# Left operands of the last three FFN2 blocks moved to the first weights' buffers, with order lists made anew

## The chip, the cores and the metric

The kernel runs on one core of one Trainium2 chip. The metric is the device time of one execution in microseconds (us), taken as the median over several runs. A profile of one execution comes with it. Engines are named as in the profile: PE (TensorE matmuls) and PEld (its weight loads), DVE (VectorE), ACT (ScalarE), POOL (GpSimd) and SP (the queue that issues nearly all DMAs).

## The reference

One transformer block with modulation: S = 2048 tokens, D = 512, attention with 32 heads in four segments, then a feed-forward part with F = 1792. Only the second part matters here:

```python
def _B_ref(x, w1, b1, w2, b2):
    h = jnp.einsum("bsd,df->bsf", x, w1) + b1
    r = jnp.where(h > 0, h, 0)
    h = r * r
    return jnp.einsum("bsf,fd->bsd", h, w2) + b2
...
h = _layernorm(x, axis=-1) * (1 + cb) + sb
x = x + gb * _B_ref(h, B_w1, B_b1, B_w2, B_b2)
```

## The kernel before

The tokens are worked through in four stages of 512 (s = 0 to 3). Attention comes first; the feed-forward part fills the second half of the run, and the attention of late stages is mixed into its start.

**Precision.** Each fp32 operand of a product is split into a rounded part and a remainder, and a product is three matmuls (high by high, high by low, low by high). "Splitting" is a cast on ACT and a subtraction on DVE.

**FFN1** (`ffn1(s, p)`, p = 0 to 6) makes 256 hidden columns for 512 tokens with a Strassen-like scheme: seven products m1 to m7 instead of eight. A product is six matmuls of 128x256 (`bh` in the profile, line 1652). DVE adds the products up (lines 1664 and 1668), ACT or DVE applies the squared ReLU (lines 1682, 1685, 1686). The result is X(s, p, i), where i = 0, 1 is the half of the tokens.

**FFN2** (`ffn2(s, i, p)`) multiplies X(s, p, i) by 256 rows of the second weights and sums over the seven blocks p in four PSUM banks, one for each *group* of products: g0 = products 1 and 6, g1 = 7 and 5, g2 = 3 and 4 (six matmuls each), g3 = product 2 (three matmuls). That is 21 matmuls for a block (`bm`, line 1737). Each block needs a left operand first:

- four sums s1 to s4 of 128x128 on POOL (line 1714);
- `hr`, the cast of three pieces (128x384) on ACT (line 1721), and `lr`, its remainder on DVE (line 1722);
- `hs`, the cast of the four sums (128x512) on ACT (line 1724), and `ls`, its remainder on DVE (line 1725).

All four splits write one buffer of the pool `ao`. It has two buffers, and one comes free when all four groups of its block are done. After the last block ten additions on DVE (lines 1769, 1771, 1773; `acc` in the code) add the four banks to two 128x512 tiles `ya` and `yb`, which hold the residual; POOL has added the bias to these (line 1752). Then they go out by DMA (line 1788). In the very last half (s = 3, i = 1) `ya` goes out in two pieces.

Which group an addition needs: a1 and a6 need g0; a7 and a5 need g1; a3 and a4 need g2; a2 needs g3. `yb` gets a1, a6, a7, a5, a4; `ya` gets a1, a6, a5, a3, a2.

**First weights.** `fetch_w1` loads w1 for FFN1 into a pool `w1` of three buffers (two inside the tile ST, one called w1c), in two pieces h = 0, 1 for each block.

**Order.** The order of the work on each engine is written out as lists of node numbers (`ORDER`); a planner (`Plan.run`) follows the list of each engine strictly and hands out buffers of the pools on the way. An engine waits at the head of its list, even when a later entry could run.

Of the kernel before, what the change touches and what calls it, by code (L numbers as in the profile page):

```python
# [17 lines left out]
P = 128  # L18
# [50 lines left out]
1113 1450-1451 1203 1211 1117-1119 1121 1362 1453 1128 1199 1454 1214 1136 1455 1124 1217 1131 1456 1359 1317 1365  # L69
# [6 lines left out]
1701 1609 1830 1704 1793 1610 1708 2051 1711 2052 1799 1716 2053 1688 2054 1806 1612 1820 1720 1833 1721-1722 1814  # L76
# [5 lines left out]
2462 2267 2463 2009 2464 2246 2243 2465 2013-2014 2249 2159 2015 2166 2162 2017 2169 1968 2178 2276 2174 2252 2599  # L82
# [15 lines left out]
3464-3465 3519 3516 3479-3481 3518 3517 3483 3482 3531 3529 3484 3528 3530 3543 3542 3751 3541 3540 3553 3750 3555  # L98
3554 3552 3749 3752 3567 3755 3565 3564 3754 3566 3576 3578 3769 3753 3577 3770 3579 3775 3771 3773 3772 3605-3607
3774 3604 3619 3616-3618 3790 3628 3631 3629 3789 3630 3791 3641 3794 3793 3642 3640 3795 3792 3643 3809 3655  # L100
3652-3654 3811 3810 3664 4099 3812 3667 4094 3676 3813-3814 3665 3677 4084 3666 3815 4089 3679 3678 3827-3831 3833
3832 3892 3890 3848 3847 3904 3845 3889 3846 3891 3901 3850-3851 3863 3866 3864-3865 3902-3903 3849 3916 3913 3867
3915 3868 3928 3914 3926-3927 3869 4134 3925 4137 4136 4135 3938 4138 3940 3937 3939 4154-4155 4157 4140 4139 4156
3950 3952 3949 3961 3951 4158 3964 4159 3962-3963 4160 4174 4176 3991 3989 3992 4177 4175 4179 3990 4003 4178 4001
4194 4004 4002 4014 4180 4016 4015 4013 4195-4196 4025 4027-4028 4197 4026 4037 4039 4212 4040 4038 4199-4200 4050
4198 4049 4052 4061 4213 4215 4214 4064 4051 4062 4216-4218 4230 4063 4232 4231 4276 4275 4235 4274 4286 4236 4277
4233 4289 4287-4288 4248 4300 4298 4301 4299 4249-4250 4253 4313 4254 4310 4325 4312 4311 4323 4322 4324 4234 4336
4334 4346 4337 4349 4335 4347-4348 4251-4252 4376 4374-4375 4377 4386 4389 4388 4387 4400 4399 4401 4398 4413 4410
4412 4411 4422 4425 4423-4424 4435-4437 4434 4446-4447 4449 4448
# [25 lines left out]
2111-2112 497 1881 1973 1976 1975 1979-1980 1972 2337 1982-1983 1987-1988 240 2133 2132 2342 2261 2260 2348 499 2344  # L135
# [23 lines left out]
700 702 471 470 609 483 608 462 461 467-468 602-603 402-403 597 599-600 855 605 861 639 606 491 629 618 630 1423-1424  # L159
# [34 lines left out]
4203 4046 4048 4058 4207 4204-4205 4060 4208 4206 4070 4220 4069 4072 4071 4211 4271 4273 4221 4225 4073-4074 4222
4226 4283 4075-4076 4078 4229 4223 4077 4285 4238-4239 4243-4244 4247 4224 4297 4295 4309 4241 4307 4319 4256-4257
4321 4261-4262 4265 4240 4331 4333 4343 4345 4242 4354 4356 4355 4357 4371 4373 4360-4361 4363 4358-4359 4383 4362
4385 4258-4260 4395 4397 4407 4409 4419 4421 4431 4433 4443 4445 4455 4454 4457 4460-4461 4463 4456 4458-4459 4462
# [14 lines left out]
2750 2413 2767 2510 2421 2420 2425 2746 2471 2443 2436 2444 2448 2748 2784-2786 2537 2794 2545 2544 2560 2549 2797  # L212
# [1623 lines left out]
```

## Time and profile before

| what | value |
|---|---|
| runs | 741.7, 743.84, 744.1 us, median 743.84 us |
| the profiled execution | 743.41 us, of it span 741.6 us |
| PE busy | 725.6 us (98% of the span) |
| DVE, POOL, ACT busy | 623.1, 493.3, 485.2 us |
| DMA | 151.82 MB, mean 205 GB/s |
| granted TensorE clock | 0.999 |

The span is what the trace covers; the profiled execution's own time is 1.8 us longer. "Busy" counts the time in which an engine had an instruction under way. A line of a timeline gives the start, the length, the engine, the line of the kernel, what is written and read, how many instructions were merged, and in square brackets how long the engine sat idle before and what ended that. The brackets stand only where the wait was worth showing.

### The profile page before, as it was taken

Reading aid. Unit: us, or ns where it says so; the run is one execution under the profiler, and the core shown is the slowest. Engines: PE = TensorE matmul, PEld = TensorE weight load, DVE = VectorE, ACT = ScalarE, POOL = GpSimd, SP = SyncE. Lnnn points to the kernel's source line nnn. Section 1 sums busy time; section 2 is a strip of 40 time slices with the busy share of each in tenths; the row PEclk is TensorE's granted clock in tenths of the full one; section 3 lists DMA queues with packets and bytes.
Section 4 is the critical chain, followed back from the end, with each engine's and each line's share of the span. In section 5 each row is a group of like instructions: output and inputs, shape, how many; then the busy total and the mean of one; then the engine's idle time right before and its main releaser. Section 6 shows DMA issues by size and latency. Waiting matters only on the chain.

```text
span 741.6 us, 20354 instructions
## 1 busy us (share of the span) xinstructions
PE 725.6 (98%) x7405; PEld 615.6 (83%) x7405; DVE 623.1 (84%) x1674; ACT 485.2 (65%) x1070; POOL 493.3 (67%) x675
## 2 busy tenths in 40 slices
PE   8999999999999999999999999999999999999996
PEld 7795777767877677775777789999999999999996
DVE  5588889898899889889998779998798877877885
ACT  3769987998879987788779654674326333643342
POOL 6767846898768787355887564766565825575672
PEclk9999999999999999999999999999999999999999
DMA  9878865437544463448673689899877667677620
GB/s 310 263 196 263 249 184 132 136 103 224 160 128 118 103 173 101 129 118 255 216 243 109 204 293 344 277 318 315 296 247 239 217 230 256 253 246 233 208 72 29
DMA packets 84606, 151.82 MB, mean 205 GB/s; under 512 B 10134, under 2 KB 32666, under 8 KB 84508
## 3 DMA queue, kind: packets, MB, share of 16 engines
q1 hardware_dynamic: 84356, 150.40, 65.0%
q8 instruction: 59, 0.97, 0.5%
q14 instruction: 39, 0.32, 0.1%
q10 hardware_dynamic: 152, 0.13, 0.1%
HBM read 94.14 MB, written 29.36 MB: 167 GB/s over the span
## 4 chain that ended last, share of the span: by engine, by line
PE 85%; DVE 5%; DMA 3%; ACT 3%; issue 1%; POOL 1%; SPq 1%; DVEq 0%; ACTq 0%; POOLq 0%
PE bm L1737 18%; PE bh L1652 18%; PE bqk L868 11%; PE bpv L1204 8%; PE ba L976 6%; PE bpb L1145 6%; PE bv L938 5%; PE bwop L1355 2%; PE bwarm L570 2%; DVE ba L981 1%; DMA ST<-w1d 1%; PE bmr L1069 1%; PE blnq L644 1%; PE blnq L653 1%; DMA ST<-sg 1%
## 5 line engine op out<-in xcount | busy, mean ns | idle before, releaser
L981 DVE CUSTOM_DVE_ANT_0 ba<-ba,msk 128x384 f32<-128x384 f32 (+2 forms) x384 | 192.9, 530 | 26.2 <-PE ba L976 16.5
L1162 ACT ACTIVATE pt<-bpb 128x512 f32<-128x512 f32 x320 | 174.7, 624 | 12.6 <-PE bpb L1145 9.7
L1149 POOL TENSOR_SCALAR_AFFINE_SELECT pt<-pt 128x512 f32<-128x512 f32 x128 | 80.6, 647 | 60.4 <-ACT pt L1162 47.1
L868 PE MATMUL bqk<-HT,WQK 64*128 64x512 f32 x720 | 106.6, 397 | 0.3 <-ACT HT L844 0.3
L1737 PE MATMUL bm<-w,ST 128*128 128x256 f32 x660 | 93.9, 283 | 0.5 <-DVE ST L1725 0.5
L1737 PEld LDWEIGHTS bm<-w,ST 128*128 128x128 f32 x660 | 85.2, 191 | 0.9 <-DVE ST L1725 0.9
L1652 PE MATMUL bh<-ST 128*128 128x256 f32 x594 | 83.4, 283 | 0.4 <-DVE ST L1446 0.4
L1204 PE MATMUL bpv<-pt,VT 128*32 128x512 f32 (+3 forms) x1024 | 82.1, 438 | 0.8 <-POOL pt L1149 0.4
L1145 PE MATMUL bpb<-ST 64*128 64x256 f32 (+2 forms) x512 | 81.5, 347 | 0.7 <-DMA ST<-mt 0.6
L868 PEld LDWEIGHTS bqk<-HT,WQK 64*128 64x128 f32 x720 | 73.4, 185 | 8.6 <-ACT HT L844 0.8
L976 PE MATMUL ba<-ST 63*128 63x256 f32 (+2 forms) x512 | 77.3, 341 | 0.9 <-DMA ST<-sg 0.6
L1652 PEld LDWEIGHTS bh<-ST 128*128 128x128 f32 x594 | 76.4, 190 | 1.3 <-DVE ST L1446 0.6
L976 PEld LDWEIGHTS ba<-ST 63*128 63x128 f32 x512 | 52.5, 185 | 20.6 <-issue 4.6
L1145 PEld LDWEIGHTS bpb<-ST 64*128 64x128 f32 x512 | 53.6, 185 | 16.5 <-issue 3.9
L1204 PEld LDWEIGHTS bpv<-pt,VT 128*32 128x32 f32 x1024 | 27.2, 109 | 33.6 <-issue 22.1
L938 PE MATMUL bv<-WVO,HT 64*128 64x512 f32 x384 | 54.6, 396 | 0.0
L981 DVE DVE_READ_ACCUMULATOR2_ANT mx<- 128x1 f32 x384 | 54.0, 141 | 0.0
L779 POOL TENSOR_TENSOR X1L<-X1L 128x512 fp32r<-128x512 f32 (+1 forms) x28 | 32.2, 1150 | 14.3 <-ACT X1L L778 12.7
L938 PEld LDWEIGHTS bv<-WVO,HT 64*128 64x128 f32 x384 | 38.6, 186 | 3.4
L1009 ACT COPY ac<-ba 128x512 f32<-128x512 f32 x64 | 35.8, 600 | 6.0 <-PE ba L976 5.4
L1020 DVE TENSOR_REDUCE mx<-ac 128x4 f32<-128x1024 f32 x32 | 38.9, 1214 | 0.1
L1652 PE MATMUL bh<-H2o,ST 128*128 128x256 f32 x252 | 35.7, 281 | 1.4 <-DMA ST<-w1d 1.0
(298 smaller groups left out, 1719.5 us busy)
## 6 DMA issues: line engine op xcount, KB each, us to landing
ST<-sg SPq DMA_DIRECT2D x192, 128.0 KB
ST<-w1d SPq DMA_DIRECT2D x21, 1024.0 KB
ST<-w1d SPq DMA_DIRECT2D x19, 768.0 KB
w1d<-X1L SPq DMA_DIRECT2D x21, 512.0 KB
w1c<-w1d SPq DMA_DIRECT2D x7, 1024.0 KB
w1c<-w1d SPq DMA_DIRECT2D x9, 768.0 KB
xt<-in_A_x SPq DMA_DIRECT2D x16, 256.0 KB
wm<-in_w_mod SPq DMA_DIRECT2D x16, 256.0 KB
```

The source lines that it names most:

```text
L868: nc.tensor.matmul(bank(banks[w]), W3(w, k, x, cols.start, cols.stop)[r], HT[r, y, k], start=first and i == 0, stop=last and i == 2)
L938: nc.tensor.matmul(bank(banks[t]), HT[r, x, k, (t2 + t) * P:(t2 + t + 1) * P], WVO[r, k, y], start=first and i == 0, stop=last and i == 2)
L976: nc.tensor.matmul(dst[:, c0:c0 + n], ST[b:b + 63, 0, sl, qt * P:(qt + 1) * P], ST[b:b + 63, 1, sl, :n], start=True, stop=True)
L981: nc.vector.tensor_tensor_reduce(i, i, msk[:, 512 - n:], scale=1.0, scalar=-3e38, op0=ALU.add, op1=ALU.max, accum_out=o)
L1009: cp = [act(512, lambda j=j: nc.scalar.copy(buf("ac", ac)[:, j], bank(keys[j])), pr[0] + 0.01 + 0.001 * j, after=[first], put=[keys[j]]) f ...
L1020: reds.append(op("DVE", 1.13, lambda: nc.vector.tensor_reduce(buf("mx", mx).rearrange("p (a t) -> p a t", t=4)[:, :, 1], acv(), axis=AX.X, ...
L1145: nc.tensor.matmul(dst, ST[b:b + 64, 1, sl, kb * P:(kb + 1) * P], ST[b:b + 64, 0, sl, q0:512], start=True, stop=True)
L1149: nc.gpsimd.affine_select(out=ap, in_=ap, pattern=[[0, ap.shape[1]], [1, P]], compare_op=ALU.is_ge, fill=0.0, base=0, channel_multiplier=-1)
L1162: ns = [op("ACT", 0.49, lambda j=j: nc.scalar.activation(buf("PPP"[n], pt)[:, i + j], bank(keys[j]), AF.Exp, scale=0.25), pr[slot] + 0.01 ...
L1204: nc.tensor.matmul(bank(o)[32 * hq:32 * hq + 32, q0:q0 + src.shape[1]], v[:, a:a + 32], src, start=start, stop=stop, tile_position=(0, 32 ...
L1652: nc.tensor.matmul(pb(i), A[:, x, kk], B[:, y, kk], start=kk == j == 0, stop=kk == 1 and j == 2)
L1737: nc.tensor.matmul(q if wide else q[:, c * HALF:(c + 1) * HALF], TL[ao][a >= 3][:, x, a_ * P:(a_ + 1) * P], LT["w2z"][:, b:15:14 - b] if w ...
```

## The change

1. In the last half (s = 3, i = 1) blocks 4, 5 and 6 write their left operand into a buffer of the pool `w1` instead of `ao`. The same four splits write it, in the same sizes, and the matmuls read it there.
2. `ORDER` is made anew. The lists agree up to small swaps until the end of stage 1 of FFN1; from there they differ on every engine. At the end PE no longer finishes block after block: it does g3 of blocks 2 to 6 last.

No instruction that computes, and no DMA, is added or removed. All lines below the lists move by one up and, from `ffn2` on, by five down (1737 becomes 1742, for example).

```diff
@@ ffn2 @@
-        ao, sk = ("ao", s, i, p), ("S", s, i, p)
+        late = s == NS - 1 and i == 1 and p >= NP - 3
+        ao, sk = ("w1" if late else "ao", s, i, p), ("S", s, i, p)
+
+        def A_(k, x):
+            if late:
+                return FF_w1(ao).rearrange("p h a k n -> p h (a k n)")[:, x, (0, 3 * P)[k]:(3 * P, 7 * P)[k]]
+            return ao_tile(ao)[k][:, x]
...
-        hr = act(384, lambda: nc.scalar.copy(ao_tile(ao)[0][:, 0], X(0, 3)), us(t0 - 5), sbuf=True, after=ready, get=[("ao", ao)])
+        hr = act(384, lambda: nc.scalar.copy(A_(0, 0), X(0, 3)), us(t0 - 5), sbuf=True, after=ready, get=[(ao[0], ao)])
...
@@ ORDER, the end of PE's list @@
-4412 4411 4422 4425 4423-4424 4435-4437 4434 4446-4447 4449 4448
+4412 4410 4422 4411 4424 4434 4436 4423 4446 4435 4447-4448 4401 4413 4425 4437 4449
```

**PE, the end of the program.** The matmuls of the last half, three for a product. The weights' name tells the block: w_7999 is block 2, w_8000 block 3, w_8001 block 4, WVO block 5, w_8795 block 6. Before:

```order
L1737 MATMUL bm<-w_8001,ao 128x256 x3
L1737 MATMUL bm<-w_8001,ST 128x256 x3
L1737 MATMUL bm<-w_8001,ao 128x256 x3
L1737 MATMUL bm<-w_8001,ST 128x256 x9
L1737 MATMUL bm<-w_8001,ao 128x256 x3
L1737 MATMUL bm<-WVO,ST 128x256 x21
L1737 MATMUL bm<-w_8795,ao 128x256 x3
L1737 MATMUL bm<-w_8795,ST 128x256 x9
L1737 MATMUL bm<-w_8795,ao 128x256 x3
L1737 MATMUL bm<-w_8795,ST 128x256 x3
L1737 MATMUL bm<-w_8795,ao 128x256 x3
```

After:

```order
L1742 MATMUL bm<-WVO,w1c 128x256 x12
L1742 MATMUL bm<-w_8001,ST 128x256 x6
L1742 MATMUL bm<-w_8795,ST 128x256 x6
L1742 MATMUL bm<-WVO,w1c 128x256 x6
L1742 MATMUL bm<-w_8795,ST 128x256 x12
L1742 MATMUL bm<-w_7999,ST 128x256 x3
L1742 MATMUL bm<-w_8000,ao 128x256 x3
L1742 MATMUL bm<-w_8001,ST 128x256 x3
L1742 MATMUL bm<-WVO,w1c 128x256 x3
L1742 MATMUL bm<-w_8795,ST 128x256 x3
```

Before, all of block 6 stood at the end, so every bank got its last matmul within the last 21. Now g0 of block 6 has 33 matmuls behind it, g1 21 and g2 15, and the last 15 are g3 of five blocks.

**DVE, the end of the program.** The last remainders of left operands and the ten additions. In the names X1L and Tx_8006 before are `ya` and `yb`; Tx_8009 and Tx_8008 are `ya` and `yb` after. Before:

```order
L1722 TENSOR_TENSOR ST<-T_6303,ST 128x384
L1725 TENSOR_TENSOR ST<-Tx_8009,ST 128x512
L1722 TENSOR_TENSOR ao<-T_6303,ao 128x384
L1725 TENSOR_TENSOR ST<-X1L,ST 128x512
L1769 TENSOR_TENSOR X1L<-bm,X1L 128x512
L1769 TENSOR_TENSOR Tx_8006<-bm,Tx_8006 128x512
L1773 TENSOR_TENSOR X1L<-bm,X1L 128x256 x4
L1769 TENSOR_TENSOR Tx_8006<-bm,Tx_8006 128x512 x2
L1773 TENSOR_TENSOR Tx_8006<-bm,Tx_8006 128x256
L1771 TENSOR_TENSOR Tx_8006<-Tx_8006,bm 128x256
```

After:

```order
L1727 TENSOR_TENSOR w1c<-X1L,w1c 128x384
L1730 TENSOR_TENSOR ST<-T_6295,ST 128x512
L1774 TENSOR_TENSOR Tx_8009<-bm,Tx_8009 128x512
L1778 TENSOR_TENSOR Tx_8009<-bm,Tx_8009 128x256
L1774 TENSOR_TENSOR Tx_8008<-bm,Tx_8008 128x512
L1778 TENSOR_TENSOR Tx_8009<-bm,Tx_8009 128x256
L1774 TENSOR_TENSOR Tx_8008<-bm,Tx_8008 128x512
L1778 TENSOR_TENSOR Tx_8009<-bm,Tx_8009 128x256
L1774 TENSOR_TENSOR Tx_8008<-bm,Tx_8008 128x512
L1778 TENSOR_TENSOR Tx_8008<-bm,Tx_8008 128x256
L1776 TENSOR_TENSOR Tx_8008<-Tx_8008,bm 128x256
L1778 TENSOR_TENSOR Tx_8009<-bm,Tx_8009 128x256
```

The ten additions are the same; they now stand as a1 ya, a6 ya, a1 yb, a5 ya, a6 yb, a3 ya, a7 yb, a5 yb, a4 yb, a2 ya, so `yb` is ready before `ya`, and the last output is the 128x256 half of `ya` instead of the whole `yb`. Both lists have all left operands ahead of the additions.

**POOL, the end of the program.** The sums for left operands (128x128) and the bias additions of the last half (128x512). Before:

```order
L1752 TENSOR_TENSOR Tx_8006<-Tx_8006,WVO 128x512
L1714 TENSOR_TENSOR Tx_8009<-T_6303 128x128
L1714 TENSOR_TENSOR Tx_8008<-X1L,Tx_8008 128x128
L1714 TENSOR_TENSOR Tx_8009<-Tx_8009,T_6303 128x128
L1752 TENSOR_TENSOR X1L<-X1L,WVO 128x512
L1714 TENSOR_TENSOR X1L<-T_6303 128x128
```

After:

```order
L1719 TENSOR_TENSOR Tx_8007<-X1L,Tx_8007 128x128
L1719 TENSOR_TENSOR Tx_8007<-X1L 128x128
L1719 TENSOR_TENSOR T_6295<-T_6295 128x128 x4
L1757 TENSOR_TENSOR Tx_8009<-Tx_8009,WVO 128x512
L1757 TENSOR_TENSOR Tx_8008<-Tx_8008,WVO 128x512
```

The two bias additions stood between the sums of blocks 3, 5 and 6; now they are the last two entries.

More of the change, by code (lines that the diff above doesn't have):

```diff
@@ L102 @@
[L102 to L106, printed above, removed]
@@ new lines @@
+3606-3607 3604 3773 3605 3616-3617 3619 3618 3789 3630 3629 3631 3628 3791 3642 3790 3794 3643 3641 3795 3640 3652
+3793 3655 3653 3792 3809 4099 3654 3810 3665 3811 4094 3812 3664 3814 3676 4089 3813 3666 3677 3667 3815 3827
+3678-3679 3828 4084 3832 3829-3831 3889 3833 3892 3890 3846 3845 3904 3847 3891 3850 3848 3851 3901 3903 3849 3902
+3863 3865 3916 3866 3864 3913-3915 3868-3869 3867 3925 3927 4135 3926 3928 4134 4136 3938 4137 3937 4138 4154
+3939-3940 4155 4140 4139 4157 4156 3952 3951 3949 3961 3963 3950 3962 3964 4159-4160 4158 4174 4176 4175 3991-3992
@@ new lines @@
+4177 3990 4178 3989 4004 4003 4196 4002 4001 4194 4179 4195 4016 4015 4180 4013-4014 4025-4026 4028 4197 4027 4038
+4040 4039 4037 4199 4049 4052 4212-4213 4200 4198 4061 4064 4218 4051 4050 4217 4062 4214 4216 4063 4275 4215 4232
+4277 4274 4230 4276 4289 4231 4235-4236 4233 4286 4288 4287 4301 4300 4299 4298 4249 4248 4250 4253-4254 4311 4313
+4312 4310 4323 4325 4322 4324 4234 4334-4335 4346 4337 4336 4251 4347 4252 4349 4348 4375 4374 4377 4376 4386-4387
+4389 4388 4400 4398-4399 4412 4410 4422 4411 4424 4434 4436 4423 4446 4435 4447-4448 4401 4413 4425 4437 4449
@@ L194 @@
[L194 to L197, printed above, removed]
+3455 3303-3304 3456 3459 3454 3306-3307 3468 3308 3716 3513 3711 3515 3469 3471 3470 3473-3474 3477 3472 3486 3527
@@ new lines @@
+3525 3487-3488 3725 3537 3489 3539 3727 3491 3549 3721 3723 3551 3492 3563 3561 3495 3734 3757 3490 3758 3760 3732
+3573 3575 3759 3729 3762 3585 3763 3587 3584 3761 3586 3588 3590 3601 3603 3589 3592 3591 3777 3613 3593 3778
+3782-3783 3779 3615 3786 3625 3627 3780 3637 3639 3651 3649 3797 4093 3766 3781 4098 3798 4088 3802 4083 3663 3803
+3799 3661 3800-3801 3673 3817 3806 3818 3675 4096 3819 3822 3684 3686 3820 4091 3688 4101 3821 3823 3685 3687 3886
+3689 3692 3690-3691 3835 3888 3693 3836-3838 3840 3900 3839 3826 3898 4086 3853 3841 3854 3858-3859 3912 3855 3862
@@ new lines @@
+3910 3844 3856 3922 3871 3857 3872 4110 3924 3874 4108 3876 3936 4114 4106 3877 3873 3934 4112 3880 3875 4142-4145
+4119 4146 4117 3958 4162 3948 3946 3960 4147 4163 4148 4164 3969 3971 4165 3970 3973 3972 3975 3974 3988 4167 3977
+4166 3986 4182 3976 3978 3998 4000 4183 4168 4184 4010 4185 4012 4186 4151 4187 4202 4022 4171 4024 4034 4203 4036
+4188 4191 4046 4204 4048 4205 4207 4060 4058 4208 4220 4069-4071 4206 4211 4271 4273 4072 4075 4073 4221 4076 4074
+4225 4077 4226 4222 4283 4078 4223 4285 4224 4229 4238-4239 4243-4244 4247 4297 4295 4309 4241 4307 4319 4240
@@ L198 @@
+4256-4257 4321 4261-4262 4265 4331 4333 4343 4345 4242 4354-4356 4371 4373 4357 4360 4358-4359 4362 4361 4363 4383
+4385 4258-4260 4395 4397 4419 4407 4409 4421 4433 4443 4431 4445 4455 4457 4454 4460 4456 4461 4458-4459 4462-4463
 """,
@@ L1720, in ffn2 @@
         s4 = sum_(3, x_[0], lambda: S_(1), ALU.subtract, [s2], put=[xk])
-        hr = act(384, lambda: nc.scalar.copy(ao_tile(ao)[0][:, 0], X(0, 3)), us(t0 - 5), sbuf=True, after=ready, get=[("ao", ao)])
-        lr = op("DVE", 0.47, lambda: nc.vector.tensor_tensor(TL[ao][0][:, 1], X(0, 3), TL[ao][0][:, 0].bitcast(F32), op=ALU.subtract),
+        hr = act(384, lambda: nc.scalar.copy(A_(0, 0), X(0, 3)), us(t0 - 5), sbuf=True, after=ready, get=[(ao[0], ao)])
+        lr = op("DVE", 0.47, lambda: nc.vector.tensor_tensor(A_(0, 1), X(0, 3), A_(0, 0).bitcast(F32), op=ALU.subtract),
                 us(t0 - 4), after=[hr], put=[xk], lock=True)
-        hs = act(512, lambda: nc.scalar.copy(TL[ao][1][:, 0], TL[sk]), us(t0 - 4), sbuf=True, after=[s1, s2, s3, s4, hr])
-        ls = op("DVE", 0.6, lambda: nc.vector.tensor_tensor(TL[ao][1][:, 1], TL[sk], TL[ao][1][:, 0].bitcast(F32), op=ALU.subtract),
+        hs = act(512, lambda: nc.scalar.copy(A_(1, 0), TL[sk]), us(t0 - 4), sbuf=True, after=[s1, s2, s3, s4, hr])
+        ls = op("DVE", 0.6, lambda: nc.vector.tensor_tensor(A_(1, 1), TL[sk], A_(1, 0).bitcast(F32), op=ALU.subtract),
                 us(t0 - 3), after=[hs], put=[sk], lock=True)
@@ L1736, in mm @@
                     wide = first and len(GRP[g]) == 2
-                    nc.tensor.matmul(q if wide else q[:, c * HALF:(c + 1) * HALF], TL[ao][a >= 3][:, x, a_ * P:(a_ + 1) * P],
+                    nc.tensor.matmul(q if wide else q[:, c * HALF:(c + 1) * HALF], A_(a >= 3, x)[:, a_ * P:(a_ + 1) * P],
                                      LT["w2z"][:, b:15:14 - b] if wide else w2slot(p)[:, y, b], start=first, stop=end)
```

64 lines of the change are left out of this document (23 added, 41 removed), and 6 rows, old and new, of the table ORDER.

## The prediction

> **What bounds the kernel now.** I read the page first, then PE's waits in the feed-forward half, then the chain of waits at the end, then the last 25 us engine by engine.
>
> ```profile
> span 741.6 us, 20354 instructions
> PE 725.6 (98%) x7405; PEld 615.6 (83%) x7405; DVE 623.1 (84%) x1674; ACT 485.2 (65%) x1070; POOL 493.3 (67%) x675
> ```
>
> PE has an instruction under way for 98% of the span, and the change leaves it all its matmuls. So only PE's pauses, and what comes after its last matmul, can be won. From 480 us on the waits of PE are these (total, times, longest):
>
> ```profile
> PE bm L1737 <- DVE ST L1725: 0.5, 1, 0.5
> PE blnq L644 <- DVE h2raw L1397: 0.5, 1, 0.5
> ```
>
> Under 1 us in 260 us. The tail is larger. The chain that ended last, and PE's own timeline there:
>
> ```profile
> 720.15 13.22 PE bm L1737 x106
> ...
> 733.40 0.69 DVE X1L L1769
> ...
> 738.19 0.33 DVEq L1832
> ```
> ```profile
> 716.11 0.64 PE L1737 MATMUL bm<-w2a,ST 128*128 128x512 f32 x3
> ...
> 718.91 0.74 PE L1737 MATMUL bm<-w,ST 128*128 128x256 f32 x5
> 720.15 2.79 PE L1737 MATMUL bm<-w,ST 128*128 128x256 f32 x19 [0.49 <-DVE ST L1725]
> ...
> 732.49 0.51 PE L1737 MATMUL bm<-w,ao 128*128 128x256 f32 x3
> 732.84 1.24 PE L1737 MATMUL bm<-w,ST 128*128 128x256 f32 x9
> 733.92 0.52 PE L1737 MATMUL bm<-w,ao 128*128 128x256 f32 x3
> 734.28 0.52 PE L1737 MATMUL bm<-w,ST 128*128 128x256 f32 x3
> 734.63 0.52 PE L1737 MATMUL bm<-w,ao 128*128 128x256 f32 x3
> ```
>
> The last five rows are block 6, whole. From 732.49 to 734.63 it issues 18 matmuls: 0.119 us each. PE's last matmul ends at 735.15; call that moment E. The span goes on for 6.45 us more. The ten additions fill the first part:
>
> ```profile
> 733.40 0.69 DVE L1769 TENSOR_TENSOR X1L<-bm,X1L 128x512 f32<-128x512 f32 x1 [1.54 <-PE bm L1737]
> 734.00 0.68 DVE L1769 TENSOR_TENSOR Tx<-bm,Tx 128x512 f32<-128x512 f32 x1
> 734.60 1.80 DVE L1773 TENSOR_TENSOR X1L<-bm,X1L 128x256 f32<-128x256 f32 x4
> 736.32 1.41 DVE L1769 TENSOR_TENSOR Tx<-bm,Tx 128x512 f32<-128x512 f32 x2
> 737.76 0.42 DVE L1773 TENSOR_TENSOR Tx<-bm,Tx 128x256 f32<-128x256 f32 x1
> 738.10 0.41 DVE L1771 TENSOR_TENSOR Tx<-Tx,bm 128x256 f32<-128x256 f32 x1
> ```
>
> DVE stood idle 1.54 us, then worked through all ten without a pause, from 733.40 to 738.51: 5.11 us, of which 3.36 us lie after E. Block 6 is the last block for all four banks, so the first bank is complete only 15 matmuls before PE ends. The rest is the last output:
>
> ```profile
> 736.48 0.33 SPq L1788 DMA_DIRECT2D out<-X1L  x1
> 738.54 0.33 SPq L1788 DMA_DIRECT2D out<-Tx  x1
> ```
> ```profile
> SPq L1832 <- DMA out<-Tx: 1.7, 1, 1.7
> ```
> ```profile
> 739.00:739.50 0.50, 0.00 (x0) 0.00 (x0) 0.00 (x0) 0.00 (x0) 0.00 (x0) 1.00 0.23 90
> 739.50:740.00 0.50, 0.00 (x0) 0.00 (x0) 0.00 (x0) 0.00 (x0) 0.00 (x0) 1.00 0.98 389
> ```
>
> `yb` (256 KB) is issued at 738.54; SP has issued it at 738.87 and waits 1.7 us, to 740.57, for the landing. Another 1.03 us ends the span. The last column of the windows is GB/s: nearly all the bytes move within 0.7 us.
>
> **The change, term 1: the tail.** Nothing is added; the same ten additions wait for banks that are complete earlier. After the change g0 of block 6 has 33 matmuls behind it: 33 x 0.119 = 3.93 us. DVE begins 0.03 us after a product's end (733.37, where the chain's PE piece ends, to 733.40), so at E - 3.90. The additions, 5.11 us in a row, then end at E + 1.21. None waits on the way: the next banks are complete at E - 2.50 (21 matmuls) and E - 1.79 (15); a5 of `ya` comes 0.69 + 0.42 + 0.68, so about 1.8 us, after the start, at E - 2.1; a3 of `ya` over a microsecond later; a2, which needs E itself, stands last, near E + 0.8. The DVE end moves from E + 3.36 to E + 1.21: 2.15 us.
>
> The output ends differently too. `yb` is complete one addition earlier, at E + 0.80; its issue ends 0.36 us later at E + 1.16, and by the row above it lands at E + 2.86. The half of `ya` (128 KB) is issued from E + 1.24 to E + 1.57. Bounds for its landing: with half of the 0.7 us of moving saved it lands at E + 2.92; if it must queue behind `yb`, 0.35 us after that, at E + 3.21. With 1.03 us behind, the span ends at E + 3.95 to E + 4.24, instead of E + 6.45. **Term 1: 2.2 to 2.5 us, taken as 2.35**, the middle, since both transfers overlap in part.
>
> **Term 2: PE's waits in the last 22 us.** Now 0.49 us at 720.15, where block 1 waits for `ls`. From there to 734.63 there are 118 matmuls (16 left of block 1, 84 of blocks 2 to 5, 18 of block 6), at 0.119 us 14.04 us, but 14.48 us passed: 0.44 us more is lost, part of it where the weight loads wait a second time:
>
> ```profile
> 720.15 2.22 PEld L1737 LDWEIGHTS bm<-w,ST 128*128 128x128 f32 x18 [0.69 <-DVE ST L1725]
> 722.55 0.19 PEld L1737 LDWEIGHTS bm<-w,ST 128*128 128x128 f32 x1 [0.18 <-DVE ST L1725]
> ```
>
> So 0.93 us is lost today. What will be lost after? Blocks 4 to 6 no longer wait for an `ao` buffer, but blocks 2 and 3 still do: block 2 takes that of block 0, block 3 that of block 1. The making of an operand costs:
>
> ```profile
> 719.00 0.51 ACT L1721 CAST ao<-X1L 128x384 fp32r<-128x384 f32 x1 [0.80 <-PE bm L1737]
> 719.42 0.61 ACT L1724 CAST ST<-X1L 128x512 fp32r<-128x512 f32 x1
> 719.94 0.63 ACT L1686 ACTIVATE T<-T 128x512 f32<-128x512 f32 x1
> ```
> ```profile
> 714.87 0.68 DVE L1725 TENSOR_TENSOR ST<-T,ST 128x512 fp32r<-128x512 f32 x1
> ...
> 718.64 1.45 DVE L1725 TENSOR_TENSOR ST<-Tx,ST 128x512 fp32r<-128x512 f32 x1
> ```
> ```profile
> 717.94 1.61 POOL L1752 TENSOR_TENSOR Tx<-Tx,WVO 128x512 f32<-128x512 f32 x1
> 720.64 0.46 POOL L1714 TENSOR_TENSOR Tx<-T 128x128 f32<-128x128 f32 x1 [1.10 <-ACT T L1686]
> ```
>
> I count from t = 0, the end of the first half's last product. Block 0 issues for 2.80 us (716.11 to 718.91, with its wide matmuls), so block 1 starts at 2.64 (the issue runs 0.16 us ahead of the end), block 2 at 5.14, and block 3, since g3 of block 2 is put off, only 18 matmuls later, at 7.28.
>
> Block 2: on ACT ahead of it stand block 1's two casts and the two ReLU steps of block 5, done at about 2.28. POOL does s1 and s2 of block 5 (which need that) before block 2's s4, which ends at 2.35 + 3 x 0.43 = 3.65. Then `hs` 3.72 to 4.33 and `ls` to 5.07, wanted at 5.14. Block 3: the buffer comes free at 5.30, `hr` to 5.86, `hs` to 6.38, `ls` to 7.12, wanted at 7.28. Both are just in time with 0.68 us for `ls`, and late by 0.2 to 0.7 us with a slow one (0.68 to 1.45). Since a delay of block 2 gives block 3 the same slack, they don't add up in full. I take 0.3 us, nearest to the fast row, as most entries of POOL there are the short 0.46 us ones; ends 0 and 1.5. Blocks 4 to 6 have over 0.3 us by the same count. **Term 2: 0.93 - 0.3 = 0.6 us gained**, ends -0.6 and +0.9.
>
> **Term 3: the rest of the new lists**, from the end of stage 1 on. Today's 0.45 us there can go or be joined by others; no row shows the new order. Ends: +0.45 and, with two more waits of the size seen, -1.0. I take 0.2 us lost.
>
> Edits costed at nothing: the splits of blocks 4 to 6 write another buffer, in the same shapes and on the same engines. Their buffers are free: the three belong to FFN1's last pieces, and the last products of FFN1 end before the first half's block 6 does. If that cover failed, block 4 would be late first. ACT's early casts of block 4 fill idle time:
>
> ```profile
> ACT ao L1721 <- PE bm L1737: 33.2, 19, 4.3
> ```
>
> **Sum:** 2.35 + 0.6 - 0.2 = 2.75 us. Against the profiled execution (743.41 us, span 741.6) that is 740.7, span 738.85. That execution is 0.43 us under the median of 743.84, so on the median it is 741.1 us, 0.37% less.
>
> **Rivals.** *New waits eat the gain.* If blocks 2 and 3 each meet slow `ls` instructions (1.5 us lost) or term 3 goes to its end, 1.1 to 1.6 us of the gain is left: about 742.4 us, no change that counts. For it speaks the slack of under 0.2 us; against it that today's list, with the same two `ao` buffers, loses 0.93 us.
>
> *The additions of the bias hold DVE.* The 718.64 `ls` ran into POOL's 128x512 addition (717.94 to 719.55) and ended 0.54 us after it. After the change both such additions stand last on POOL, behind block 6's sums, at about 9.4 to 12.0, and `ls` of block 6 is ready to start at 10.1. If both go first, `ls` ends at 12.7, wanted at 12.99: the point of harm is 0.3 us away. With block 6 a further 1.3 us late (one addition) the time is 742.1 us. The Trainium skill ("SBUF — State Buffer", section "Who interferes with whom") states the rule: a VectorE instruction with two SBUF inputs and a GpSimd one that reads SBUF take a shared port pair in turn, and the later one fully blocks. The trace agrees, with 1.45 against 0.68 us. By that rule the harm comes only if block 6's sums are late.
>
> *Slower: the last piece of first weights lands late.*
>
> ```profile
> 691.50 0.34 SPq L1788 DMA_DIRECT2D out<-Tx  x1
> 696.30 0.52 SPq L1579 DMA_DIRECT2D ST<-w1d  x1
> ```
> ```profile
> 433.22 0.96 PE L1652 MATMUL bh<-H2o,ST 128*128 128x256 f32 x6 [0.96 <-DMA ST<-w1d]
> ```
>
> On SP the fetch of block 6's larger piece now stands behind an output that waits for DVE's last addition of stage 2; before it stood ahead. A late fetch did stop PE once, for 0.96 us. To turn the change to slower, PE must lose 2.75 + 2.2 = 5 us, a fetch later than its need by five times that wait: about 746 us. Against it: 132 matmuls (15.7 us) lie between the start of FFN1's block 6 and t = 0, and E is t = 17.8, so that block begins 33.5 us before E, near 701.6, and the output went at 691.50 in this trace.
>
> **How the numbers follow.** Forecast 0.56, new waits 0.25, bias additions 0.08, late fetch 0.08; the rest, 0.03, small gains on either side. A difference of 0.3% (2.2 us) is about what runs of this kernel can tell from none. The sum is only 0.5 us beyond it, and the two middle rivals lie within. So faster 0.57, same 0.34, slower 0.09. Range: best 743.84 - 2.5 - 0.9 - 0.45 = 740.0, opened to 739.8 for the runs' own scatter; at the other end 2.2 - 0.6 - 1.0 leaves 0.6 us, so 743.2, opened to 743.4.
>
> **What would show it.** The first addition starts near 3.9 us before PE's last matmul ends, the last DVE instruction ends 1.2 us after it, and the span 4.1 us after it. If DVE ends later than E + 1.6, term 1 is wrong; if brackets on PE's last 147 matmuls hold more than 0.9 us, term 2; if PE waits between 480 and 712 us hold more than 1 us, term 3.

## The result, and the profile after

| | before | after |
|---|---|---|
| median of the runs | 742.64 us (6 runs) | 738.50 us (6 runs) |
| the profiled execution | 743.41 us, span 741.6 | 738.22 us, span 736.5 |
| ratio to before, 95% interval | | 0.9943 [0.9928, 0.9958] |

The change makes the kernel 0.57% faster, 4.1 us; two later series against before gave ratios of 0.9932 [0.9916, 0.9948] and 0.9931 [0.9904, 0.9957]. Over all series the runs of before lie near 743.4 us and those of after near 738.4, so the change is worth about 5 us where 2.75 was forecast; the time lies 1.3 us below the range. Three disturbed executions (779.83 us in e5_swap, 2081.11 us in e9_g0_first, and the only one of e15_before_again, 982.95 us at a granted clock of 0.655) are left out of every median and ratio below.

The head of the page after:

```profile
span 736.5 us, 20355 instructions
PE 725.5 (98%) x7405; PEld 614.5 (83%) x7405; DVE 622.5 (85%) x1674; ACT 486.2 (66%) x1070; POOL 493.1 (67%) x675
```

PE's busy time is what it was (725.5 against 725.6 us) for the same 7405 matmuls, so the 5.1 us of span came out of idle time. The tail, on PE, DVE and SP's queue:

```profile
729.01 1.96 PE L1742 MATMUL bm<-w,ST 128*128 128x256 f32 x15
730.81 0.52 PE L1742 MATMUL bm<-w,ao 128*128 128x256 f32 x3
731.17 0.52 PE L1742 MATMUL bm<-w,ST 128*128 128x256 f32 x3
731.53 0.52 PE L1742 MATMUL bm<-WVO,w1c 128*128 128x256 f32 x3
731.89 0.51 PE L1742 MATMUL bm<-w,ST 128*128 128x256 f32 x3
```
```profile
728.57 0.69 DVE L1774 TENSOR_TENSOR Tx<-bm,Tx 128x512 f32<-128x512 f32 x1 [1.87 <-PE bm L1742]
729.29 0.42 DVE L1778 TENSOR_TENSOR Tx<-bm,Tx 128x256 f32<-128x256 f32 x1
729.63 0.68 DVE L1774 TENSOR_TENSOR Tx<-bm,Tx 128x512 f32<-128x512 f32 x1
...
732.55 0.41 DVE L1776 TENSOR_TENSOR Tx<-Tx,bm 128x256 f32<-128x256 f32 x1
732.88 0.42 DVE L1778 TENSOR_TENSOR Tx<-bm,Tx 128x256 f32<-128x256 f32 x1
```
```profile
733.02 0.81 SPq L1793 DMA_DIRECT2D out<-Tx  x2
```
```profile
SPq L1837 <- DMA out<-Tx: 1.6, 1, 1.6
```

PE's last matmul ends at 732.40 (E). The first addition starts 3.83 us before it, the last ends at 733.30, E + 0.90, and the span ends at E + 4.10 instead of E + 6.45. In PE's rows from the last half's start (714.28) to its end there is no bracket, where before one of 0.49 us stood.

To see where the rest came from, I take the start of the same matmul, counted from the program's first, in both traces: number 4800 lies near the start of FFN1, 4960 and 5100 some 20 and 41 us later, 7258 is the first of the last half.

| stretch | before | after | difference |
|---|---|---|---|
| to matmul 4800 (attention) | 412.91 | 413.59 | +0.68 |
| 4800 to 4960 | 20.64 | 18.73 | -1.91 |
| 4960 to 5100 | 20.97 | 20.97 | 0 |
| 5100 to 7258 (FFN1 and FFN2 up to the last half) | 261.59 | 261.00 | -0.59 |
| 7258 to E (last half) | 19.05 | 18.12 | -0.93 |
| E to the end of the span | 6.45 | 4.10 | -2.35 |
| sum | 741.6 | 736.5 | -5.10 |

The span is printed to 0.1 us, so the stretch from E to the end is good to 0.05 us.

The largest item beside the tail, 1.91 us near 430 us, lies in a place where the forecast looked for nothing. PE there, before:

```profile
428.57 1.58 PE L1652 MATMUL bh<-ST 128*128 128x256 f32 x11 [0.37 <-DVE ST L1446]
```

and the 0.96 us at 433.22 that the prediction quotes for its slower rival. Counted from the start of the row ahead of each pause to the start of the row behind it, the two places take 0.64 and 1.21 us longer than after the change, 1.85 of the 1.91 us. After the change both rows stand without a bracket, and the only bracket of the stretch is one that both kernels have:

```profile
420.88 0.85 PE L1651 MATMUL bh<-H2o,ST 128*128 128x256 f32 x5 [0.42 <-POOL H2o L1445]
...
428.47 1.67 PE L1651 MATMUL bh<-ST 128*128 128x256 f32 x12
...
432.08 0.86 PE L1651 MATMUL bh<-H2o,ST 128*128 128x256 f32 x6
```

SP's queue in that place, first before and then after (its longest wait, and the DMAs behind it):

```profile
SPq L813 <- DVE X1L L1262: 8.9, 1, 8.9
```
```profile
421.59 0.38 SPq L813 DMA_DIRECT2D W2s<-in_B_w  x1
...
425.29 0.57 SPq L1579 DMA_DIRECT2D ST<-w1d  x1
```
```profile
SPq L812 <- DVE X1L L1261: 5.2, 1, 5.2
```
```profile
419.84 0.38 SPq L812 DMA_DIRECT2D W2s<-in_B_w  x1
...
423.77 0.57 SPq L1578 DMA_DIRECT2D ST<-w1d  x1
```

The load into W2s (raw second weights) waits for a DVE instruction of one and the same line of code, 1262 before and 1261 after, but for another of its instructions. Before, that is the one that starts at 420.74; after, the second of the pair that starts at 418.40, seven instructions earlier in DVE's list:

```profile
417.74 1.28 DVE L1262 TENSOR_TENSOR X1L<-X1L,am 128x512 f32<-128x512 f32 x2
...
420.74 0.69 DVE L1262 TENSOR_TENSOR X1L<-X1L,am 128x512 f32<-128x512 f32 x1
```
```profile
418.40 1.28 DVE L1261 TENSOR_TENSOR X1L<-X1L,am 128x512 f32<-128x512 f32 x2
```

So the load goes out 1.75 us earlier, and the fetch of first weights behind it on the queue 1.52 us earlier. It is this fetch, issued at 425.29, that PE waited for at 433.22. Nothing in the diff names the load. One of the small swaps in attention does it: on SP, the store of a normalised attention tile (node 1418) and two gather loads (2229, 2230) stand in another order. The planner hands out buffers of the attention pool as it goes through the lists, so with the swap later tiles get other buffers, and the W2s tile, which lies over memory of that pool, waits for another instruction. That the buffers are the link is read from the code; that the swap does it is what e5_swap tests.

### The profile page after: what moved, and what is told of

Same layout as the page of the kernel before. It is cut to its first block, busy times and chain, and to the rows that moved or that the text cites. A ratio compares the mean times of both kernels' runs of the same rounds, so it can differ in the third digit from the quotient of the medians.

```text
span 736.5 us, 20355 instructions
## 1 busy us (share of the span) xinstructions
PE 725.5 (98%) x7405; PEld 614.5 (83%) x7405; DVE 622.5 (85%) x1674; ACT 486.2 (66%) x1070; POOL 493.1 (67%) x675
## 4 chain that ended last, share of the span: by engine, by line
PE 49%; DVE 2%; issue 1%; DMA 0%; ACT 0%; SPq 0%; POOL 0%; DVEq 0%; ACTq 0%; POOLq 0%
PE bm L1742 19%; PE bh L1651 19%; PE bwop L1354 2%; PE bpv L1203 2%; PE bpb L1144 1%; PE bwop L1308 1%; PE bwop L1307 1%; PE bwop L1306 1%; PE blnq L643 1%; PE bwot L1331 1%; PE ba L975 1%; DVE ba L980 1%; DMA ot<-o_dram 0%; DVE Tx L1778 0%; DVE WVO L1299 0%
## 5 line engine op out<-in xcount | busy, mean ns | idle before, releaser
L909 POOL TENSOR_SCALAR e<-e 128x512 f32<-128x512 f32 x24 | 35.8, 1491 | 1.8 <-ACT e L905 1.4
```

Source lines behind the costliest of these rows:

```text
L909: m_ = op("POOL", 1.57, lambda e=e: nc.gpsimd.tensor_scalar(TL[e], TL[e], 1.0, None, op0=ALU.min), p2 + 0.002, after=[x1_])
```

## The experiments

My theory after the result: three separate things, the tail (2.35 us), no pause in the last half (0.93), and the swap in attention (1.9). Rivals: the gain near 430 us is chance, or comes from another part of the lists; the late buffers themselves do it; the new order of FFN1 and FFN2 as a whole is needed. All times are medians. The series ran on different chips, so a kernel is compared with before by the ratio within its own series. Stretches as above, from one profile each:

| kernel | median us (runs) | ratio to before, 95% | 4800-4960 | 5100-7258 | last half | E to end |
|---|---|---|---|---|---|---|
| e1_after_again | 738.39 (6) | 0.9932 [0.9916, 0.9948] | 18.78 | 261.64 | 18.12 | 4.07 |
| e2_tail_only | 740.68 (12) | 0.9971 [0.9951, 0.9991] | 20.53 | 262.43 | 19.19 | 4.01 |
| e3_block_tail | 740.78 (10) | 0.9957 [0.9941, 0.9973] | 18.75 | 261.03 | 18.13 | 6.59 |
| e4_old_head | 740.83 (7) | 0.9959 [0.9943, 0.9976] | 20.48 | 261.83 | 18.12 | 4.10 |
| e5_swap | 742.87 (11) | 0.9993 [0.9978, 1.0008] | 18.78 | 264.15 | 19.03 | 6.47 |
| e6_late_only | 743.26 (10) | 0.9992 [0.9972, 1.0013] | 20.39 | 262.01 | 18.90 | 6.52 |
| e7_adds_last | 743.04 (12) | 1.0002 [0.9985, 1.0019] | 20.28 | 261.38 | 18.40 | 6.62 |
| e9_g0_first | 738.25 (5) | 0.9930 [0.9903, 0.9958] | 18.77 | 261.00 | 18.25 | 3.77 |
| e10_sum | 738.49 (6) | 0.9938 [0.9914, 0.9962] | 18.79 | 260.84 | 18.17 | 4.11 |
| e13_sum_no_swap | 738.89 (10) | 0.9945 [0.9929, 0.9962] | 20.28 | 261.16 | 18.18 | 4.10 |
| e14_swap_again | 742.08 (12) | 0.9977 [0.9957, 0.9997] | 18.78 | 263.27 | 19.03 | 6.51 |
| e16_sum_again | 739.08 (8) | 0.9935 [0.9910, 0.9960] | 18.78 | 263.47 | 18.16 | 4.12 |
| e17_no_swap_again | 739.78 (12) | 0.9941 [0.9922, 0.9960] | 20.46 | 261.74 | 18.15 | 4.13 |
| e18_after_third | 738.20 (8) | 0.9931 [0.9904, 0.9957] | 18.78 | 261.86 | 18.12 | 4.09 |

In the edits, `moved` puts the named nodes of a list into the order given and leaves all others in their places.

**The tail alone, and everything but the tail.** e2_tail_only is the kernel before with the late buffers and three pieces of the new lists:

```diff
+ORDER["PE"] = moved(ORDER["PE"], [4400, 4398, 4399, 4412, 4410, 4422, 4411, 4424, 4434, 4436, 4423, 4446, 4435, 4447, 4448, 4401, 4413, 4425, 4437, 4449])
+ORDER["DVE"] = moved(ORDER["DVE"], [4455, 4457, 4454, 4460, 4456, 4461, 4458, 4459, 4462, 4463])
+ORDER["SP"] = moved(ORDER["SP"], [4464, 4466])
```

> The lists of before everywhere, with the first weights' buffers for blocks 4 to 6; only PE's products of blocks 2 to 6 of the last half, the ten additions and the two last outputs of SP stand in the changed kernel's order. Theory (the tail carries 2.36 us, the rest comes from the remade lists): the span ends 4.1 us after PE's last matmul, PE keeps its pause of about 0.5 us at block 1 and the one near 611 us, the time is 2.4 us under before, near 740.2 us. Rival (the group order and the free buffers bring all, the lists nothing): 738.5 us, no pause in the last 22 us.

e3_block_tail is the kernel after with these three pieces in the order of before.

> The changed kernel with before's tail: PE's products of blocks 2 to 6 block after block, the additions and last outputs in before's order; all other lists as changed. Theory: the first addition starts 1.8 us before PE's last matmul ends, the span goes on 6.4 us after it, no pauses of PE in the last 22 us, 2.3 us over the changed kernel, near 740.9 us. Rival (the tail's order is not what matters, since the output's landing ends the span): within 0.5 us of the changed kernel.

DVE's end of the list in e3_block_tail:

```profile
730.22 1.29 DVE L1784 TENSOR_TENSOR Tx<-bm,Tx 128x512 f32<-128x512 f32 x2 [4.01 <-PE bm L1752]
731.42 1.80 DVE L1788 TENSOR_TENSOR Tx<-bm,Tx 128x256 f32<-128x256 f32 x4
733.14 1.41 DVE L1784 TENSOR_TENSOR Tx<-bm,Tx 128x512 f32<-128x512 f32 x2
...
734.92 0.41 DVE L1786 TENSOR_TENSOR Tx<-Tx,bm 128x256 f32<-128x256 f32 x1
```

It ends 3.43 us after PE (3.36 before), and the tail is back at 6.59 us; the last half stays at 18.13 without a pause. In e2_tail_only the tail is 4.01 us while the pause in the last half stays (19.19 us). So the order of PE's last products, the additions and the outputs is worth 2.4 to 2.5 us in either setting (medians: e3 against e1 2.39, e2 against before 2.5, its series of before at 743.21; means 1.9 and 2.3), the same with and without the other lists as far as these runs can tell.

**The kernel after again, and after with the early swaps undone.**

> The changed kernel once more. If the pauses of PE before 440 us differ by chance from run to run, the profile shows others than before (a pause of 0.3 to 1 us at another place, the start of FFN1 moved by up to 1 us), while from 480 us on PE has no pause again, the last matmul is followed by 4.1 us and the first addition starts 3.9 us ahead of it. Time 738.0 to 739.5 us.

It took 738.39 us. The pauses near 430 us are missing again, which speaks against chance; but from 480 us on PE did wait once, 0.4 us for first weights.

e4_old_head puts the entries that differ ahead of stage 1's end back:

```diff
+ORDER["PE"] = moved(ORDER["PE"], [1199, 1454, 1688, 2054, 2243, 2465])
+ORDER["ACT"] = moved(ORDER["ACT"], [2348, 499, 2344])
+ORDER["DVE"] = moved(ORDER["DVE"], [483, 608])
+ORDER["POOL"] = moved(ORDER["POOL"], [2425, 2746])
+ORDER["SP"] = moved(ORDER["SP"], [2229, 1418, 2230, 2733, 2805])
```

> The changed kernel with the handful of entries that were swapped in attention (six of PE, three of ACT, two of DVE, two of POOL, five of SP) put back as before. Theory (pauses before 440 us are chance): the same time as the changed kernel, within 0.5 us. Rival (the swaps removed the pauses of 0.37 and 0.96 us near 428 and 433 us): both pauses are back, the time is 1.2 us over the changed kernel.

```profile
433.13 0.98 PE L1663 MATMUL bh<-H2o,ST 128*128 128x256 f32 x6 [1.18 <-DMA ST<-w1d]
```
```profile
SPq L824 <- DVE X1L L1273: 8.9, 1, 8.9
```

The larger pause (1.18 us) and SP's wait of 8.9 us are back; the smaller one of 0.37 us has no bracket. The median is 2.44 us above e1_after_again, the mean 1.9. The early swaps, which I had priced at nothing, carry a good part of the gain; the runs below put the three SP entries alone lower.

**The pieces by themselves, in the kernel before.** e5_swap has only

```diff
+ORDER["SP"] = moved(ORDER["SP"], [2230, 2229, 1418])
```

> The kernel before with three neighbouring entries of SP's list in another order (the store of a normalised attention tile goes behind two loads of gathered queries instead of between them), as in the changed kernel; nothing else. Theory (this swap hands other buffers of the attention pool to later tiles, so that the second weights' raw tile, which lies over that pool, waits for an earlier DVE instruction): the first load of that tile is issued near 419 us instead of 421.6, PE's pauses of 0.37 us near 428 and 0.96 us near 433 are gone, the stretch from the start of FFN1 to 433 us takes 18.8 us instead of 20.6, and the time is 1.5 to 2 us under before. Rival (another of the swaps did it): the load near 421.6 us, both pauses there, the time of before.

Near 430 us it does what the theory says: the stretch takes 18.78 us, and the load waits 5.2 us, here for the remainder two instructions ahead of the one it waits for in the kernel after:

```profile
SPq L821 <- DVE ST L1454: 5.2, 1, 5.2
```

But the median is only 0.6 us below before. Its profile has PE waits after 480 us that the profile of before has not:

```profile
PE bh L1660 <- DMA ST<-w1d: 1.5, 2, 0.7
PE bh L1660 <- DMA w1c<-w1d: 0.2, 1, 0.2
```

e6_late_only has the late buffers with the lists as before.

> The kernel before with the left operands of the last three blocks in the first weights' buffers, all order lists as before. Theory (the buffers gain nothing while the lists hold every engine to the old order): the span's end 6.4 us after PE's last matmul and PE's pause of 0.5 us at block 1 as before, the time within 0.5 us of before. Rival (waits for the two buffers cost time by themselves): the last 22 us shorter by 0.4 us or more.

743.26 us, tail 6.52: the buffers alone buy no time that these runs can tell (0.9972 to 1.0013). By the code they are what lets g3 of blocks 2 to 6 stand last: an `ao` buffer comes free only after all four groups of its block, so with two of them blocks 4 to 6 would wait for the end. That was not run.

e7_adds_last moves POOL's two bias additions behind the last sums:

```diff
+ORDER["POOL"] = moved(ORDER["POOL"], [4426, 4405, 4427, 4438, 4429, 4428, 4439, 4441, 4440, 4451, 4453])
```

> The kernel before with POOL's two bias additions of the last half moved behind all sums, as in the changed kernel; nothing else. Theory (one of them held DVE's ls of block 1 for 0.8 us): that ls takes 0.7 us, PE's pause of 0.49 us at block 1 and the second wait of the weight loads are gone, and from the start of the last half to PE's last matmul it takes 18.1 us instead of 19.05. Rival (the pause comes from waiting for the ao buffer): 19.0 us as before. The time is 0.9 us under before by the theory.

The time does not show the 0.9 us: 0.45 us in the median, nothing in the ratio. In the profile the last half is 0.65 us shorter (18.40 against 19.05, where 18.1 was expected) and has no bracket. The `ls` that took 1.45 us before:

```profile
717.62 0.68 DVE L1733 TENSOR_TENSOR ST<-Tx,ST 128x512 fp32r<-128x512 f32 x1
```

and POOL beside it:

```profile
716.49 0.45 POOL L1722 TENSOR_TENSOR X1L<-X1L 128x128 f32<-128x128 f32 x1
719.62 0.52 POOL L1722 TENSOR_TENSOR Tx<-T 128x128 f32<-128x128 f32 x1 [2.67 <-ACT T L1694]
```

POOL is idle while it runs, and it takes 0.68 us. This is the conflict that the prediction read from the row at 718.64, and the rule that it cited there from the Trainium skill ("SBUF — State Buffer", section "Who interferes with whom") agrees: 1.45 us beside a bias addition, 0.68 without. It was today's pause, not a coming one. About half of what is left over the 18.1 us has the same cause: with the old order of PE and DVE, block 6's `ls` now falls beside the second bias addition (729.11 to 730.71), and PE's row behind it takes 0.15 us longer than before.

```profile
729.49 1.77 DVE L1733 TENSOR_TENSOR ST<-X1L,ST 128x512 fp32r<-128x512 f32 x1
```

**The count of block 2, tried the other way.** e8_add_early puts one bias addition back into the kernel after, ahead of block 5's sums:

```diff
+ORDER["POOL"] = moved(ORDER["POOL"], [4451, 4426, 4427, 4393, 4429, 4428, 4438, 4440, 4439, 4441, 4453])
```

> The changed kernel with the bias addition of ya put on POOL ahead of block 5's sums, which stand ahead of block 2's last sum. Theory (block 2 has little slack): block 2's last sum, hs and ls come 1.3 us later, PE pauses 0.5 to 1.3 us at block 2, and the last half takes 18.6 to 19.4 us instead of 18.1. Rival (the slack of block 2 is over a microsecond): 18.1 us and no pause.

```profile
715.56 1.29 POOL L1765 TENSOR_TENSOR Tx<-Tx,WVO 128x512 f32<-128x512 f32 x1
717.41 0.78 POOL L1727 TENSOR_TENSOR Tx<-X1L 128x128 f32<-128x128 f32 x1 [0.56 <-DVE ao L1735]
```

One run, 738.91 us. The last half grew from 18.12 to 18.42 us, less than expected: POOL had been idle for 1.54 us at this place, and the addition fits into that. What it did delay is the remainder `lr` on DVE beside it (0.84 instead of 0.55 us), and with it block 5's first sum, 0.28 us later from the start of the last half. That 0.3 us of it came through to PE shows that block 2 has hardly any slack.

**Two products earlier.** e9_g0_first:

```diff
+ORDER["PE"] = moved(ORDER["PE"], [4434, 4446, 4436, 4423, 4435])
```

> The kernel after, with the g0 products of block 6 moved up by two products in PE's list, so that 39 matmuls instead of 33 stand behind the first complete bank. If the tail is set by DVE's ten additions in a row (4.73 us from the moment that the first bank is complete), DVE ends nearer to PE's last matmul by up to 0.7 us, but not before the last addition can start (it needs the last matmul and takes 0.41 us): 0.45 us after E instead of 0.89, and the span ends 3.65 us after E instead of 4.1; time 0.4 us below the kernel after. Rival: block 6's left operand is not ready that early, and PE waits up to 0.3 us for it, so that nothing is left.

The tail falls to 3.77 us and the last half grows by 0.13; what is left, 0.2 us where 0.4 was expected, is too little for the median to show (738.25).

**The pieces added up.** e10_sum is e2_tail_only with the swap and the bias additions last; e13_sum_no_swap is the same without the swap.

> The lists before with three small pieces of the change put together: late buffers with the reordered tail (PE's last products, ten additions, two outputs), the three swapped SP entries in attention, and the two bias additions last on POOL. If the causes add up: 1.9 us less between matmul 4800 and 4960 (18.75 us), a tail of 4.0 us after E instead of 6.44, a last half of 18.1 to 18.4 us instead of 19.05; together 4.9 us less than before, 738.4 us, which is the time of the kernel after. Rival: the time won at 433 us is given back to first-weight fetches at 611 to 655 us as in the profile with the three swapped entries alone; then 107.5 us between matmul 6300 and 7200 becomes 109 to 110 us, and the time is 739.5 to 740.

> The sum kernel of three pieces without the three swapped SP entries: the lists before, late buffers with the reordered tail, bias additions last. If the swapped entries are worth the 1.9 us of the pauses near 433 us also in the median, this is 1.9 to 2.4 us above the sum kernel: 740.4 to 740.9 us, with 20.3 to 20.7 us between matmul 4800 and 4960. If they are worth only the 0.5 us that they gave alone, 739 us.

e10_sum has the time of the kernel after as far as these runs can tell, with 46 named entries of four lists in place of five new lists. But e13_sum_no_swap is hardly slower, though its pause stands in the profile:

```profile
432.23 0.98 PE L1670 MATMUL bh<-H2o,ST 128*128 128x256 f32 x6 [0.81 <-DMA ST<-w1d]
```

So both were run again with the kernel after on one chip, and the swap alone once more.

> The three swapped SP entries alone once more, with a second profile. If the 1.5 us missing from their gain were chance on the first chip, it is 741.4 us, 1.9 below the kernel before, and the profile shows no waits for first weights at 625 and 655 us. If the swapped entries move the fetches into waits, the same waits stand in this profile and the time is again 0.5 us below before.

> The sum kernel again, on one chip with the next two. With the three swapped SP entries the stretch from matmul 4800 to 4960 takes 18.8 us. If the swap is worth its 1.5 us in the median: 1.5 us below the sum without the swap. If it is worth nothing in the median (given back elsewhere): the same within 0.5 us.

> The sum kernel without the three swapped SP entries again: 20.3 us from matmul 4800 to 4960, 1.5 us above the sum kernel if the swap counts, the same as it if not.

> The kernel after on the same chip. If the rest of its remade lists is worth nothing, it has the time of the sum kernel within 0.5 us; if the lists save the waits at 611 to 655 us that profiles of the lists before show by chance, it is up to 1 us below it, and its runs scatter less.

The swap alone gave 1.3 us this time; in the sum kernel 0.7 (739.08 against 739.78); the kernel after is 0.9 below the sum kernel, and its runs do not scatter less (735.99 to 741.41 against 737.05 to 740.59). Of these only the swap alone is clear of noise, and barely (0.9957 to 0.9997). In the profiles the stretch 4800 to 4960 takes 18.73 to 18.79 us in all twelve with the swap (the two of SP's whole list below among them) and 20.28 to 20.64 in all seven without it, 1.7 us apart.

All series together say more than one. For each kernel I take the mean of its runs against the mean of before in the same series, and fit one price for each piece, the prices adding up, to these 14 differences (the result and all rows of the table but e9_g0_first). The tail comes out at 2.5 us, the bias additions last at 1.0, the swap at 1.2 and the rest of the new lists at 0.2, with standard errors of 0.35 to 0.5 us. The fit counts e4_old_head as the kernel after without the swap, though that edit undoes the early swaps of the other lists too. So the three small pieces carry nearly all of the 5 us, and the rest of the new lists cannot be told from nothing.

Whether some of the swap's 1.7 us is lost again further on is not shown. With the other lists as before, the four profiles with the swap average 262.93 us from 5100 to 7258, and the six without it 261.72; with the lists of after and the swap six average 261.42 (e8_add_early with 262.0 among them). But two profiles of the one sum kernel differ by more than these averages, 260.84 and 263.47 us. In the profile of e14_swap_again the longer stretch is a single row, a wait for first weights:

```profile
501.18 1.62 PE L1660 MATMUL bh<-H2o,ST 128*128 128x256 f32 x12 [1.50 <-DMA ST<-w1d]
```

Kernels without the swap have such waits too (1.0 us in e6_late_only). Which transfers push the late fetch is in no row, and stays open.

**SP's new list without the others.** e11_sp_after is the kernel before with SP's whole list from after; e12_sum_sp the sum kernel with it.

> The kernel before with SP's whole list taken from the kernel after, everything else as before. If the order of SP's later entries (where the fetches of the first weights stand among outputs and copies of the residual) is what keeps the kernel after free of waits at 611 to 655 us, the 1.9 us won at 433 us stay: 741.4 us, with no wait for first weights after 600 us. Rival: these waits come from the work of the other engines or by chance; then it is like the three swapped entries alone, 742.5 to 743.

> The sum kernel (late buffers, reordered tail, bias additions last) with SP's whole list taken from the kernel after. If SP's order of fetches keeps the gain at 433 us: 738.3 us and 107.6 us between matmul 6300 and 7200. If the lists of the other engines are needed for that: the same time as the sum kernel with the three swapped entries, or up to 1 us more where SP's new order meets the old order of DVE and ACT.

Both were far off: 765.04 us, ratio 1.0296 [1.0268, 1.0324], and 761.32 us, 1.0248 [1.0218, 1.0278]. SP and PE in e11_sp_after:

```profile
SPq L1395 <- DVE ST L1733: 11.0, 1, 11.0
```
```profile
597.73 0.32 SPq L1395 DMA_DIRECT2D Tx<-x_dram  x1
598.46 0.52 SPq L1587 DMA_DIRECT2D ST<-w1d  x1
```
```profile
604.71 1.62 PE L1660 MATMUL bh<-H2o,ST 128*128 128x256 f32 x6 [9.20 <-DMA ST<-w1d]
```

A load of the residual waits 11 us for a remainder (`ls`) that DVE, on its old list, makes late; the fetch of first weights stands right behind it, and PE stops for 9.2 us. Later waits of 3.1 and 3.6 us follow. Neither theory had this. It is the prediction's slower rival, reached from the other side: a fetch behind an entry that waits. So SP's new list is good only with other new lists beside it. That DVE's would be enough was not run.

e15_before_again, the kernel before once more, was to show both pauses a second time.

> The kernel before, a second profile. The pauses near 433 us (0.37 and 0.96 us) and at block 1 of the last half (0.49 us) should stand in it again, since they follow from the order of the lists; the pause of 0.45 us at 611 us need not.

It gave no answer, so for the kernel before itself the pauses rest on one profile. The six other kernels without the swap have at least the larger one.

## Why the prediction was wrong in size, by its own steps

- **Term 1, the tail: right.** 2.35 us forecast, 2.35 measured in the profiles (6.45 to 4.10), 2.39 and 2.5 in medians. The path to it was off by 0.2 to 0.5 us on both sides, and that the two errors cancel is luck: the ten additions take 4.73 us in a row, not 5.11, so DVE ends at E + 0.90 instead of E + 1.21; what follows then takes 3.2 us instead of 2.7 to 3.0.
- **Term 2, PE in the last half: mechanism right, mis-sized.** The 0.93 us lost before was counted correctly and all of it went (19.05 to 18.12). The 0.3 us that I took off for new waits did not come: no bracket stands in the last half. The two `ls` that I feared slow ran fast:

```profile
719.07 0.69 DVE L1730 TENSOR_TENSOR ST<-X1L,ST 128x512 fp32r<-128x512 f32 x1 [0.27 <-ACT ST L1729]
...
720.94 0.69 DVE L1730 TENSOR_TENSOR ST<-Tx,ST 128x512 fp32r<-128x512 f32 x1
```

  The bias additions, which had made one slow, now lie behind the sums (e7_adds_last). The slack was as small as I counted (e8_add_early). In the runs the piece is worth 1.0 us by the fit, where 0.6 was forecast.
- **Term 3, the rest of the lists: the step that failed.** It was taken as 0.2 us lost with ends of -1.0 and +0.45, from the waits after 480 us and from the end of stage 1 on. The early swaps were left without a price. One of them, three entries of SP, takes away 1.91 us in the two profiles and 1.2 us by the fit over all series (e4_old_head, with all early swaps undone, 2.44 us above e1_after_again); the prediction even quoted the 0.96 us pause that went, as evidence for its slower rival, without asking whether the change could end it. The stretch from 5100 to 7258 gave 0.59 us more in these two profiles, less than two profiles of one kernel differ there. With the sizes measured the sum is 2.35 + 0.93 + 1.91 + 0.59 = 5.8 us in these two profiles, of which attention took back 0.7.
- **The miss as a sum.** The forecast of 741.1 us lies 2.6 us above the 738.5 us measured. By the fit, an estimate, 1.6 us of that is term 3 (0.2 us lost against 1.2 + 0.2 gained), 0.4 us term 2 and 0.15 us term 1. The other 0.4 us is the starting point: 743.84 us was the median of three runs, and over all series before lies near 743.4.
- **Rivals.** New waits did not eat the gain. The time that the prediction set beside this rival was too high: by its own terms slow `ls` in blocks 2 and 3 leave 2.35 - 0.6 - 0.2 = 1.6 us and the end of term 3 leaves 1.95, not 1.1. Block 6 did not run late behind the bias additions: its `ls` started while the first of them was under way and took 1.11 us, with no bracket on PE after it. No fetch came late in the profile after; e1_after_again has one wait of 0.4 us.

```profile
725.58 1.11 DVE L1730 TENSOR_TENSOR ST<-T,ST 128x512 fp32r<-128x512 f32 x1 [1.01 <-ACT ST L1729]
```
```profile
724.86 2.99 POOL L1757 TENSOR_TENSOR Tx<-Tx,WVO 128x512 f32<-128x512 f32 x2
```

- **What was to show it.** The first addition started 3.83 us before E (3.9 said), the span ended 4.10 after E (4.1 said). The test for term 3, PE waits of more than 1 us between 480 and 712 us, looked in the wrong stretch.

## What to carry to other kernels

Where a planner hands out buffers while it follows lists, a swap of three DMAs in one place changes which instruction a load elsewhere waits for. So when lists are made anew, price every pause of the trace as one that may go, also in parts that "agree up to small swaps", and look in the built program at what the loads ahead of each pause wait for. The tail, which nothing else touches, could be counted row by row from the trace before. The swap's gain stands in every profile, but its worth in time needed all series together: one pair of kernels put it at 0.4 us (e13_sum_no_swap against e10_sum), another at 2.4 (e4_old_head against e1_after_again).

## What the runs showed of the hardware

- Four 128x256 additions from PSUM into one tile in a row took 1.72 us on DVE, 0.43 each (731.42 to 733.14 in e3_block_tail, as before); standing between 128x512 additions into the other tile they took 0.34 each (729.29 to 729.63 after). That is the 0.38 us by which the new order of the ten shortened them.
- A DVE remainder of 128x512 takes 0.68 us while POOL is idle, 1.11 to 1.78 us where a 128x512 addition of POOL runs beside it (1.77 at 729.49 in e7_adds_last, 1.78 at 723.15 before). The slow ones end at nearly the same distance behind that addition: 0.54 and 0.56 us before (720.09 behind 719.55, 724.93 behind 724.37), 0.55 in e7_adds_last (731.26 behind 730.71).
- The profiles differ by up to 6 us at matmul 4800 (410.96 to 416.72), and two of one and the same kernel by 4.6 (416.72 in e10_sum, 412.11 in e16_sum_again). Waits for first weights come and go in one and the same kernel: e16_sum_again has one of 0.6 us after 480 us and e10_sum none, e14_swap_again one of 1.5 us and e5_swap two of 1.5 us together. A single pause of this size in one profile is no property of the kernel; one that stands in all seven may be.
